# Holding back early score units in one batch, ranking an addition first, and moving six small copies, in a fused attention and mixer kernel

## The chip, the cores and the metric

The kernel runs on one core of one Trainium2 chip. A core has TensorE (PE) for matrix products, VectorE (DVE), ScalarE (ACT), GpSimd (POOL) and SyncE (SP). Each engine works through its own queue in order. SP and POOL also start transfers (DMA) here. The metric is the device time of one execution in microseconds (us), as the median of several runs. Lower is better.

## The reference

Eight batches of 3008 rows are computed. An attention-like stage without softmax gates u, and a mixer (first over the rows, "tokens", then over the columns, "channels") follows it:

```python
scores = (1.0 / S) * np.matmul(z, z.transpose(0, 2, 1))   # z: 8 x 3008 x 64
attn = np.maximum(scores, 0.0) ** 2
x = u * np.matmul(attn, v)                                # u, v: 8 x 3008 x 256
h = np.maximum(x.transpose(0, 2, 1) @ w_tok1, 0.0) @ w_tok2      # 256 tokens inside
u2 = x + h.transpose(0, 2, 1)
out = u2 + np.maximum(u2 @ w_ch1, 0.0) @ w_ch2            # 1536 channels inside
```

## The kernel before

**Tiles and blocks.** The rows of a batch are cut into six blocks of 512 (the last has 448). A block (b, q) is the 512 query rows q of batch b; it needs the squared relu of its scores against all six groups g of 512 key rows. The scores are symmetric, so a block (b, q) with q > g is not computed again: the tile of (b, g, q) is turned by DMA transposes (`flip`, L562) and used a second time. Tiles on the diagonal (`triangle`) are computed only on and above the diagonal, and their lower part is filled by three small transposes (`flip_tiles`, L554).

**Score units.** The list `units` (L332) holds every (b, q, g) in the order in which it is to be scored, in two halves `pr`, each of which is two matmuls of 512 columns (L465) into one pair of PSUM banks. ScalarE applies the relu (L503, on the diagonal L491) into one of six `at` tiles, and VectorE squares it in place (L511, on the diagonal L542). From there on a tile is ready for the product with v (`av_matmul`, L692), or for its transposes into one of eleven `fl` tiles. `score_run` sends units to TensorE in the order of the list; `can_score` says how many of the next ones may go (their z is turned, and an `at` tile is free in the plan).

**PSUM.** From the second block on there are four pairs of banks (`ring`). A block holds two of them for its accumulators acc0 and acc1, a score unit, a token product, a channel product or a mixer output holds one until an engine has emptied it.

**The end of a block.** `finish` (L804) copies the upper half of an accumulator on ScalarE (L820), adds it to the lower half on VectorE (L826), which frees the pair, and multiplies by u (`gate`, L846). SP turns the result (`turn_x`, L884), and VectorE makes four differences of it (`x_sums`, L921), which the fast form of the token product reads.

**The mixer of a batch.** `tok1` (L1029) sums up the token product over the batch; `tok2` (L1086) multiplies back into six tiles h_ps, and `add` (inside `tok2`, L1095, the token addition) adds each to xT on VectorE; `ch1` (L1143) makes the hidden channels hp from xT, and ScalarE, at times VectorE, applies the relu into h2pre (L1181, L1183). The second channel product is either plain (`ch2`, L1365) or in a form with seven instead of eight products (`product`, L1279), for which VectorE makes sums hsum of h2pre (`make_sums`, L1222 to L1234); seven collections (L1316) add the products to the result ro. The last 64 rows of two batches share one plain product: `keep_ends` (L1151) copies them from h2pre into the tile hs, with six copies for each batch, on GpSimd (L1155).

**The order.** All this is interleaved by a planner that runs when the program is built (the loop at L1742). It keeps an estimate of TensorE's time (`pe[0]`) and of when each engine is free, and picks for TensorE a score run, a half of an AV group, or a mixer piece. Work of VectorE, ScalarE and SP is put in by `push(engine, ready, busy, lat, fn, first)`; `next_op` (L372) takes the operation with the smallest key `(start, -first, ready)`, so `first` decides between operations that could start at the same time. The squares (L493, L505), the sums and the token addition have first=0, the accumulator's addition and the gate first=1. What an operation's function emits beside it, as `keep_ends` does, is put into the queues at the point at which the planner issues that operation, without a cost of its own. The engines' real order is then fixed, and the semaphores make it safe.

`goals` (L1733) sets when mixer pieces may come. Batch 0's token sum (L1029) comes before block (1,2), and its six token products with the channel work of its first three tiles before block (1,3). The rest of batch 0's mixer comes before block (2,0), together with the first half of batch 1's, and so on from batch to batch. At the boundary that the change touches, TensorE's order is: last products of block (1,2), six token products mixed with the first channel products, plain channel products, then blocks (1,3), (1,4) and (1,5), and the next mixer stretch.

The lines in the loop that choose the number of units to be scored:

```python
runs = blk is not None and blk.whole
most = RING if runs else 1
n = can_score(done_units, most)
slots = sorted(d.t for d, _ in ring if d.t is not None)
n_now = min(n, len(slots))
```

Of the kernel before, what the change touches and what calls it, by code (L numbers as in the profile page):

```python
# [57 lines left out]
def kernel(  # L58
# [11 lines left out]
    nc = tc.nc  # L70
    B, S, D = u.shape
# [9 lines left out]
    NQ = (S + QW - 1) // QW  # L81
# [8 lines left out]
    first = ctx.enter_context(ExitStack())  # L90
# [97 lines left out]
    def bank_pair(slot, name):  # L188

        if slot == RING and not last_psum:  # L190
            first.close()
            last_psum.append(ctx.enter_context(
                tc.tile_pool(name="last_psum", bufs=1, space=bass.MemoryType.PSUM)))
        pool = psum if slot < RING else last_psum[0]
        return pool.tile([P, 2, QW], F32, tag=f"ps{slot}", name=name, bufs=1)
# [122 lines left out]
    def key_order(b, q):  # L318

        direct = [g for g in range(LAST) if direct_block(b, q, g)]  # L320
        flipped = [g for g in range(LAST) if not direct_block(b, q, g)]
        first = (b, q) == (0, 0)
        made = direct + [LAST] if first else direct[:1] + [LAST] + direct[1:]
        order = []
        while direct or flipped:
            order += direct[:1] + flipped[:1]
            del direct[:1], flipped[:1]
        order.insert(LAST if first else 2, LAST)
        return made, order


    units = [((b, q, g), pr) for b in range(B) for q in range(NQ)  # L332
             for g in key_order(b, q)[0] for pr in range(GK // 2)]
# [22 lines left out]
    ring = [(Done(0.0), i) for i in range(RING)]  # L356
# [7 lines left out]
    def push(engine, ready, busy, lat, fn, first=0, room=(), done=None, frees=()):  # L364
        op = Op(ready, busy, lat, fn, first, room, done, frees)
        waiting[engine].append(op)
        return op.done

    def has_room(names):
        return names() if callable(names) else all(live[n] < ROOM[n] for n in names)  # L370
# [65 lines left out]
    def can_score(first_unit, most):  # L436

        n, at = 0, live["at"]
        for (b, q, g), pr in units[first_unit:first_unit + most]:
            if (b, q) not in turned or (b, g) not in turned:  # L440
                break
            at += pr == 0
            if at > ROOM["at"]:
                break
            n += 1
        return n
# [493 lines left out]
    def take_slot():  # L940
        slot = min((s for s in ring if s[0].t is not None), key=lambda s: s[0].t)
        ring.remove(slot)
        return slot[1], slot[0].t
# [55 lines left out]
    def add_mixer(b):  # L999
# [80 lines left out]
        def tok2(q, end):  # L1080
            slot, _ = take_slot()
            W = widths[q]
            h = bank_pair(slot, "h_ps")
            for dh in range(DT):
                for th in range(2):
                    nc.tensor.matmul(  # L1086
                        h[:, dh, :W], st["a"][:, th, dh * P:(dh + 1) * P],
                        w_tok2_sb[:, th, q * QW:q * QW + W], start=(th == 0), stop=(th == 1))

            def add(t):  # L1090

                xT = xTs[b, q]
                n = full_tiles[q]
                to = xT[:, :, :n * P].rearrange("p h (t s) -> p h t s", t=n)
                nc.vector.tensor_add(  # L1095
                    to, to, h[:, :, :n * P].rearrange("p h (s t) -> p h t s", t=n))
                if n * P < W:
                    to = xT[:, :, n * P:W]
                    nc.vector.tensor_add(to, to, h[:, :, n * P:W])
                if W < QW and b % 2:  # L1100

                    nc.gpsimd.tensor_copy(xT[:, :, W:], xT[:, :, W - TAIL:W])
                    t += 0.5
                u_done[q].t = t
                st["turned", q] = push("sp", t, 1.25, 5.5, lambda t: turn_u2(q, t), first=1,
                                       room=lambda: has_room(("us",)) and (
                                           q <= HALF or goal[0] > (b, 1 + HALF)))
            ring.append((push("dve", end + 0.21, 1.12, 1.25, add), slot))

        def turn_u2(q, t):  # L1110
            live["us"] += 1
# [18 lines left out]
        def ch1(q, c2, borrowed, end):  # L1130
            slots = [take_slot()[0] for _ in range(1 + ((b, q, c2) == VERY_LAST))]
            W = widths[q]
            xT = xTs[b, q]
            if c2 % 2 == 0:
                live["h2"] += 1
                st["h2", q, c2 // 2] = sb.tile(
                    [P, 4, QW], BF16, tag="h2", name="h2pre", bufs=ROOM["h2"])
            hps = [bank_pair(slot, "hp") for slot in slots]
            hp = hps[0]
            for r in range(2):  # L1140
                cc = 2 * c2 + r
                for dc in range(DT):
                    nc.tensor.matmul(  # L1143
                        hps[r % len(hps)][:, r, :W], w_ch1_sb[:, dc, cc * P:(cc + 1) * P],
                        xT[:, dc, :W], start=(dc == 0), stop=(dc == DT - 1))
            h2 = st["h2", q, c2 // 2][:, 2 * (c2 % 2):2 * (c2 % 2) + 2, :]

            def load(e):
                return max(free[e], end) + sum(op.busy for op in waiting[e])

            def keep_ends():  # L1151
                if c2 == 0 and b % 2 == 0:
                    pair["hs"] = sb.tile([P, CHT, P], BF16, tag="hs", name="hs", bufs=1)
                r = b % 2 * TAIL
                nc.gpsimd.tensor_copy(  # L1155
                    pair["hs"][:, 2 * c2:2 * c2 + 2, r:r + TAIL], h2[:, :, W - TAIL:W])

            if (b, q, c2) == VERY_LAST:
                landed, freed = [], Done()

                def evacuate_part(r, t):
                    if r:
                        nc.scalar.activation(h2[:, r, :W], hps[1][:, r, :W], ACT.Relu)
                    else:
                        nc.vector.tensor_single_scalar(h2[:, r, :W], hp[:, r, :W], 0.0, AX.max)
                    landed.append(t)
                    if len(landed) == 2:
                        h2_done[q, c2].t = freed.t = max(landed)
                        keep_ends()

                for r, engine, at, busy in ((0, "dve", end - 0.18, 0.62), (1, "act", end + 0.21, 0.5)):
                    push(engine, at, busy, busy + 0.16, lambda t, r=r: evacuate_part(r, t))
                ring.extend((freed, slot) for slot in slots)
                release("xT", xT_uses[q])
                return
            on_act = load("act") + 0.92 < load("dve") + 1.15 + (b > 0)

            def evacuate(t):
                recent[0] = h2[:, 0, :1]
                if on_act:  # L1180
                    nc.scalar.activation(h2[:, :, :W], hp[:, :, :W], ACT.Relu)  # L1181
                else:
                    nc.vector.tensor_single_scalar(h2[:, :, :W], hp[:, :, :W], 0.0, AX.max)  # L1183
                if q == NQ - 1:
                    keep_ends()
                if fast(q) and c2 % 2:
                    if borrowed and q == HALF and b < B - 1:
                        late_sums.append(lambda t: make_sums(q, c2 // 2, t))
                    else:
                        make_sums(q, c2 // 2, t)  # L1190
            engine, busy = ("act", 0.92) if on_act else ("dve", 1.15)
            ring.append((push(engine, end + 0.21, busy, busy + 0.16, evacuate,
                              done=h2_done[q, c2]), slots[0]))
            if c2 == CHT // 2 - 1:
                release("xT", xT_uses[q])
# [150 lines left out]
        def fast(q):  # L1346

            return (b > 0 or q >= HALF) and (b, q) != (B - 1, NQ - 1)
# [62 lines left out]
        for q in range(NQ):  # L1411
            heads.append(Piece(0.784, [x_done[b, NQ - 1], xd_done[b, q], tok_mix_done],
                               lambda end, q=q: tok1(q, end),
                               opens=q < NQ - 1, closes=q > 0, key=(b, 0), joins=q == 0 and b > 0))
        for q in range(NQ):
            heads.append(Piece(4 * column_time(widths[q]), [a_done, tok2_done[q]],
                               lambda end, q=q: tok2(q, end), key=(b, 1)))
# [318 lines left out]
    done_units = 2  # L1736
# [5 lines left out]
    while cur[0] is not None or heads or tails:  # L1742
# [4 lines left out]
        blk = cur[0]  # L1747
# [11 lines left out]
        runs = blk is not None and blk.whole  # L1759
        most = RING if runs else 1  # L1760
        n = can_score(done_units, most)
        slots = sorted(d.t for d, _ in ring if d.t is not None)
        n_now = min(n, len(slots))
        ts = FAR
# [115 lines left out]
```

## Time and profile before

| what | value |
|---|---|
| median of three runs | 1122.46 us (1120.7 to 1124.12) |
| the profiled execution | 1119.13 us |
| its span, first to last instruction | 1117.2 us |
| TensorE busy | 1108.2 us, 99% |
| VectorE busy | 782.6 us, 70% |
| ScalarE busy | 655.4 us, 59% |
| GpSimd busy | 164.6 us, 15% |
| mean granted clock of TensorE | 0.999 |
| HBM, read and written | 65.40 and 24.64 MB, 81 GB/s |

A line of the timeline gives the start from the beginning of the span, the duration, the engine, the source line and the operation, the tile written and the tiles read, the shape, and in brackets the idle time of the engine before it with what ended it. A group "x4" is four instructions of one kind that follow each other. The matmuls are pipelined: one of 512 columns is listed with some 0.37 us, but the next one starts about 0.22 us after it, or about 0.11 us in the products L465 and L692, where two use half of the array each. So the starts tell the pace, not the durations. In the same way ScalarE's relu of 1024 elements is listed with 1.02 us, and three of them in a row take 2.85 us. Batch 0's blocks and the first blocks of batch 1 fill the span up to about 128 us; the first mixer stretch of batch 0 lies from there to 168 us; blocks (1,3) to (1,5) follow until 201 us; then the next mixer stretch. That one lasts until 272 us. From there on the blocks of a batch and a mixer stretch follow each other, with a period of some 136 us, and the last batch's mixer ends near 1112 us.

### The profile page before, as it was taken

To read this page: it belongs to the slowest core of one execution; us is meant where nothing else is said; L and a number is where in the kernel's file an instruction comes from. 1 tells how busy PE (TensorE), PEld (TensorE's weight loads), DVE (VectorE), ACT (ScalarE), POOL (GpSimd) and SP (SyncE) were. 2 spreads that over 40 slices of the span, in tenths; PEclk is the share of its full clock that TensorE was granted. 3 is DMA by queue.
4 is the path that set the end of the run, shared out by engine and by line. 5 is a ranking of instruction groups with operands and counts; after the bars stand their busy time and mean duration, and the time that the engine had idled before them with its cause. 6 is when DMAs were issued, how large, how long until landed. Compare 5 with 4: busy or idle time off the path is not lost.

```text
span 1117.2 us, 26931 instructions
## 1 busy us (share of the span) xinstructions
PE 1108.2 (99%) x10965; PEld 682.2 (61%) x10965; DVE 782.6 (70%) x1850; ACT 655.4 (59%) x816; POOL 164.6 (15%) x388
## 2 busy tenths in 40 slices
PE   9999999999999999999999999999999999999998
PEld 3444466766557665576555865557655676556776
DVE  6889756875758757588565885578756787557764
ACT  8998525535855458545675456653676536743453
POOL 5320110221003110031000311003200220000000
PEclk9999999999999999999999999999999999999999
DMA  9999954687877959779596897968978678685123
GB/s 178 173 182 160 201 115 109 123 178 139 179 130 151 184 132 185 131 147 210 124 184 117 151 196 143 167 123 162 192 150 172 115 152 168 132 159 105 53 71 82
DMA packets 466155, 165.51 MB, mean 148 GB/s; under 512 B 433072, under 2 KB 449008, under 8 KB 466032
## 3 DMA queue, kind: packets, MB, share of 16 engines
q1 hardware_dynamic: 436640, 131.11, 56.5%
q0 software_dynamic: 28880, 32.32, 20.4%
q8 instruction: 85, 1.39, 0.5%
q10 hardware_dynamic: 512, 0.38, 0.1%
q14 instruction: 38, 0.31, 0.1%
HBM read 65.40 MB, written 24.64 MB: 81 GB/s over the span
## 4 chain that ended last, share of the span: by engine, by line
PE 97%; DMA 1%; DVE 1%; ACT 0%; issue 0%; POOL 0%; ACTq 0%
PE acc L692 41%; PE hp L1143 22%; PE xb L1279 10%; PE zb L1279 7%; PE sc L465 6%; PE a_ps L1029 3%; PE h_ps L1086 3%; PE op L1365 3%; PE first_acc L609 1%; DMA fl<-at 1%; DMA v_sb<-in_v_dram 0%; DVE a_f L1045 0%; PE wp L205 0%; DVE xT L1095 0%; DVE a_f L1049 0%; DVE a_f L1057 0%
## 5 line engine op out<-in xcount | busy, mean ns | idle before, releaser
L1181 ACT ACTIVATE h2pre<-hp 128x1024 bf16<-128x1024 f32 (+1 forms) x276 | 268.6, 1007 | 258.4 <-PE hp L1143 172.7
L692 PEld LDWEIGHTS <-v_sb 64*128 64x128 bf16 x4418 | 244.4, 94 | 213.0
L692 PE MATMUL acc<-at,v_sb 64*128 64x512 bf16 (+1 forms) x2738 | 339.9, 374 | 0.0
L503 ACT ACTIVATE at<-sc 128x1024 bf16<-128x1024 f32 (+1 forms) x290 | 288.1, 1027 | 79.7 <-PE sc L465 72.7
L511 DVE TENSOR_TENSOR at<-at 128x1024 bf16<-128x1024 bf16 (+1 forms) x290 | 198.6, 688 | 114.6 <-ACT at L503 110.0
L1143 PE MATMUL hp<-xT,w_ch_sb 128*128 128x512 bf16 (+1 forms) x1152 | 273.3, 375 | 0.1
L692 PE MATMUL acc<-fl,v_sb 64*128 64x512 bf16 (+1 forms) x1680 | 191.1, 367 | 0.0
L1143 PEld LDWEIGHTS <-w_ch_sb 128*128 128x128 bf16 x1152 | 106.2, 98 | 99.8 <-issue 3.0
L465 PE MATMUL sc<-zT 64*128 64x512 bf16 (+1 forms) x732 | 131.6, 359 | 0.1
L1279 PEld LDWEIGHTS <-hsum 128*128 128x128 bf16 x1944 | 115.9, 98 | 16.8
L1279 PEld LDWEIGHTS <-h2pre 128*128 128x128 bf16 x1458 | 89.1, 98 | 19.3 <-issue 1.2
L820 ACT COPY cp<-acc 128x512 f32<-128x512 f32 (+1 forms) x94 | 54.8, 583 | 62.8 <-PE acc L692 50.4
L826 DVE TENSOR_TENSOR cp<-acc,cp 128x512 f32<-128x512 f32 (+1 forms) x94 | 63.5, 676 | 35.4 <-ACT cp L820 34.6
L491 ACT ACTIVATE at<-sc 128x512 bf16<-128x512 f32 (+3 forms) x152 | 56.2, 443 | 47.2 <-PE sc L465 44.5
L1222 DVE TENSOR_TENSOR hsum<-h2pre 128x512 bf16<-128x512 bf16 (+1 forms) x132 | 52.7, 403 | 39.0 <-ACT h2pre L1181 38.5
L1316 DVE TENSOR_TENSOR ro<-xb,u_sb 128x256 f32<-128x256 f32 (+1 forms) x132 | 52.8, 400 | 24.0 <-PE xb L1279 22.2
L542 DVE TENSOR_TENSOR at<-at 128x512 bf16<-128x512 bf16 (+3 forms) x152 | 41.7, 322 | 39.8 <-ACT at L491 39.8
L1279 PE MATMUL xb<-w_mix_sb,hsum 128*128 128x128 bf16 x972 | 68.6, 219 | 0.0
L465 PEld LDWEIGHTS <-zT 64*128 64x128 bf16 x732 | 42.4, 94 | 41.5 <-issue 3.9
L124 POOL CAST mark<-at 128x1 f32<-128x1 bf16 x24 | 7.7, 320 | 377.0 <-DVE at L511 377.0
L846 DVE TENSOR_TENSOR xT<-cp,uT 128x512 bf16<-128x512 f32 (+1 forms) x94 | 62.4, 664 | 0.8
L1095 DVE TENSOR_TENSOR xT<-xT,h_ps 128x1024 bf16<-128x1024 bf16 (+1 forms) x48 | 54.7, 1173 | 4.7 <-PE h_ps L1086 4.6
(88 smaller groups left out, 988.0 us busy)
## 6 DMA issues: line engine op xcount, KB each, us to landing
out_dram<-ro SPq DMA_DIRECT2D x37, 512.0 KB, 2.9
v_sb<-in_v_dram POOLq DMA_DIRECT2D x40, 256.0 KB, 4.6
ur<-in_u_dram POOLq DMA_DIRECT2D x40, 256.0 KB, 5.1
w_tok_sb<-in_moe_w_tok_dram POOLq DMA_DIRECT2D x10, 256.0 KB, 10.7
zs<-in_z_dram POOLq DMA_DIRECT2D x35, 64.0 KB, 3.6
at<-at SPq DMA_TRANSPOSE x114, 2.4
out_dram<-ro SPq DMA_DIRECT2D x7, 256.0 KB, 2.2
fl<-at SPq DMA_TRANSPOSE x105, 4.2
```

What stands on the lines that cost most here:

```text
L465: nc.tensor.matmul(sc[:, r, c0:c1], zT[h, k:k + P], zT[h, m + c0:m + c1], start=True, stop=True)
L491: nc.scalar.activation(a3[:, i, c0:c1], sc[:, r, c0:c1], ACT.Relu, scale=inv_S)
L503: nc.scalar.activation(view, sv, ACT.Relu, scale=inv_S)
L511: nc.vector.tensor_mul(view, view, view)
L692: nc.tensor.matmul(o, vs[blk.b, g][rows, i, dh * P:(dh + 1) * P], rhs, start=(dh, h) not in blk.begun, stop=stop, skip_group_check=True)
L820: nc.scalar.copy(cp[:, :W], acc[:, 1, :W])
L826: nc.vector.tensor_add(cp[:, :W], acc[:, 0, :W], cp[:, :W])
L846: nc.vector.tensor_mul(xT[:, dh, :full * P].rearrange("p (t s) -> p t s", s=P), acc[:, :full * P].rearrange("p (t s) -> p t s", s=P), uT[: ...
L1095: nc.vector.tensor_add(to, to, h[:, :, :n * P].rearrange("p h (s t) -> p h t s", t=n))
L1143: nc.tensor.matmul(hps[r % len(hps)][:, r, :W], w_ch1_sb[:, dc, cc * P:(cc + 1) * P], xT[:, dc, :W], start=(dc == 0), stop=(dc == DT - 1))
L1181: nc.scalar.activation(h2[:, :, :W], hp[:, :, :W], ACT.Relu)
L1279: nc.tensor.matmul(to[:, i * P:(i + 1) * P], lhs, weights[:, c2, :], start=(first_use and c2 == 0 and i == 0), stop=(c2 == CHT // 2 - 1), ...
```

## The change

Three edits. (1) While TensorE's current block is in batch 1, a score unit is only sent if it belongs to the current block or to the next one; units further on are held (for block (1,5), the next one is (2,0)). (2) The token addition is pushed with first=2 instead of 0, ahead of everything else on VectorE in the planner's ties. (3) In the last batch, the six copies into hs are VectorE's instead of GpSimd's.

```diff
@@ tok2 @@
-            ring.append((push("dve", end + 0.21, 1.12, 1.25, add), slot))
+            ring.append((push("dve", end + 0.21, 1.12, 1.25, add, first=2), slot))
@@ keep_ends @@
                 r = b % 2 * TAIL
-                nc.gpsimd.tensor_copy(
+                copier = nc.gpsimd if b < B - 1 else nc.vector
+                copier.tensor_copy(
                     pair["hs"][:, 2 * c2:2 * c2 + 2, r:r + TAIL], h2[:, :, W - TAIL:W])
@@ the planner's loop @@
         n = can_score(done_units, most)
+        if n and blk is not None and blk.b == 1:
+            b, q, _ = units[done_units][0]
+            if b * NQ + q > NQ + blk.q + 1:
+                n = 0
         slots = sorted(d.t for d, _ in ring if d.t is not None)
```

The changed kernel has the same instructions on TensorE and SP as before. One hp relu goes from VectorE to ScalarE, and the six copies from GpSimd to VectorE. TensorE's order differs in two places only: at the end of block (1,2), where the first half of unit (1,4,4) is no longer scored ahead of the mixer stretch, and in blocks (1,3) to (1,5), where the units of (1,5) and (2,0) come later. On the other engines the order differs in the same stretch, at the token additions of each batch (one sum hsum, L1227, comes after the last addition instead of before it), and at the six copies.

## The prediction

> **What bounds the kernel now.** I read the page's busy shares and its chain of waits first, then what TensorE waited for, and then the timeline of each engine around the places where the order of the changed kernel differs. On the page, TensorE is the bound, at full clock:
>
> ```profile
> span 1117.2 us, 26931 instructions
> PE 1108.2 (99%) x10965; PEld 682.2 (61%) x10965; DVE 782.6 (70%) x1850; ACT 655.4 (59%) x816; POOL 164.6 (15%) x388
> PEclk9999999999999999999999999999999999999999
> PE 97%; DMA 1%; DVE 1%; ACT 0%; issue 0%; POOL 0%; ACTq 0%
> ```
>
> So only TensorE's own stalls can be won, and only new ones can be lost. What it waited for, in the whole span, is a handful of waits, three of them at one line, the token product L1086:
>
> ```profile
> PE h_ps L1086 <- ACT at L491: 0.9, 1, 0.9
> PE h_ps L1086 <- DVE xT L1095: 0.7, 1, 0.7
> PE xb L1279 <- DVE ro L1316: 0.7, 4, 0.2
> PE h_ps L1086 <- DVE cp L826: 0.2, 1, 0.2
> ```
>
> The timeline of TensorE shows where (start, duration, engine, line, operation, count, idle before it):
>
> ```profile
> 128.09 1.90 PE L1086 MATMUL h_ps<-w_tok_sb,a_sb 128*128 128x512 bf16 x8
> 130.85 1.02 PE L1086 MATMUL h_ps<-w_tok_sb,a_sb 128*128 128x512 bf16 x4 [0.86 <-ACT at L491]
> 132.06 1.02 PE L1086 MATMUL h_ps<-w_tok_sb,a_sb 128*128 128x512 bf16 x4 [0.18 <-DVE cp L826]
> 133.19 1.02 PE L1143 MATMUL hp<-xT,w_ch_sb 128*128 128x512 bf16 x4
> 134.92 1.02 PE L1086 MATMUL h_ps<-w_tok_sb,a_sb 128*128 128x512 bf16 x4 [0.71 <-DVE xT L1095]
> 135.78 1.03 PE L1143 MATMUL hp<-xT,w_ch_sb 128*128 128x512 bf16 x4
> 136.64 0.92 PE L1086 MATMUL h_ps<-w_tok_sb,a_sb 128*128 128x448 bf16 x4
> 137.40 2.97 PE L1143 MATMUL hp<-xT,w_ch_sb 128*128 128x512 bf16 x13
> ```
>
> Four matmuls of 512 columns take 0.86 us from start to start (134.92 to 135.78), of 448 columns 0.76 (136.64 to 137.40). From 128.09 to 137.40 there are seven groups of the first kind and one of the second: 7 x 0.86 + 0.76 = 6.78 us of work in 9.31, so 2.5 us of stall (1.04 before 130.85, 0.35, 0.27, and 0.87 before 134.92). What made it is on ScalarE and VectorE:
>
> ```profile
> 129.82 0.98 ACT L491 ACTIVATE at<-sc 128x512 bf16<-128x512 f32 x2 [2.22 <-DMA fl<-at]
> 130.69 0.59 ACT L820 COPY cp<-acc 128x512 f32<-128x512 f32 x1
> 130.45 0.74 DVE L542 TENSOR_TENSOR at<-at 128x512 bf16<-128x512 bf16 x2 [1.52 <-ACT at L491]
> 131.31 0.69 DVE L826 TENSOR_TENSOR cp<-acc,cp 128x512 f32<-128x512 f32 x1
> 131.92 1.21 DVE L1095 TENSOR_TENSOR xT<-xT,h_ps 128x1024 bf16<-128x1024 bf16 x1
> 133.05 0.69 DVE L846 TENSOR_TENSOR xT<-cp,uT 128x512 bf16<-128x512 f32 x1
> ```
>
> The relu of unit (1,4,4), scored last before the mixer, waits 2.22 us for an at buffer that a transpose still reads. Behind it stand the copy of the second accumulator on ScalarE, and on VectorE the unit's squares, that accumulator's addition, and the first token addition. Two of the four PSUM pairs stay taken meanwhile.
>
> **The hold.** In TensorE's order the first half of (1,4,4) moves behind the mixer stretch, to the place where its second half is; the two score matmuls cost the same there (0.2 us), so this moves work and removes none. Its place is now free: ScalarE's copy L820 no longer waits. The accumulator's last matmuls end near 128.0; copy to 128.6; VectorE, after L511 (127.64) and L846 (128.25), starts L826 near 128.9 and the first L1095 near 129.5 instead of 131.92. The second L846 (0.69) now stands behind all six additions. Additions follow each other every 1.14 us (132.00 to 133.13 in the chain; the group of five took 5.47). So the pair of addition k is free at 130.6, 131.8, 132.9, 134.1. TensorE at rate would ask, with three pairs free at the start: fourth h_ps at 130.5 (pair of the accumulator, free at 129.6), first hp 131.4 (130.6), fifth h_ps 132.2 (131.8), next hp 133.1 (132.9), last h_ps 134.0 (134.1, or the first hp's pair, relu done by 133.6). Each is met with 0.1 to 0.9 us in hand: the stall goes, -2.5 us. From below: if additions start 1 us later than this, each of these asks waits in turn, about 1.0 us in all comes back, -1.5. I take -2.4.
>
> What is late next: in batch 1 the units of two blocks ahead are no longer scored early. In the changed order, the blocks (1,3) and (1,4) run nearly without scores, and all twelve units of (2,0) stand inside block (1,5), 11.2 us at rate (94 matmuls of 448 columns, two to 0.187, and the scores). ScalarE has there two copies left from (1,4) (0.59 each), the triangle pair (1.52 for four, row 171.40), ten relus at 0.93 (two back to back took 1.95 at 169.52) and two copies of 0.53: 13.1 us, so it falls behind by up to 1.9, and it then takes all six of the hp relus that follow, where VectorE took one before. Two pairs are for scores: a relu starts 0.46 after its score (184.26 to 184.72) and a pair is asked for again two units, 1.92 us, later, against 0.46 + 1.02 = 1.48, so the lag is taken up by 0.4 us per pair and by the first accumulator's copy, which stands ahead of the last two relus. Ends: 0 and +1.9 us; nearest to the row of 169.52, I take +0.2.
>
> The transposes move too. On SP's queue the first two of (1,4,4)'s transposes (135.81 and 139.80, 1.2 us each) leave their place beside the two u_sb transposes and come after the mixer stretch; those of (1,5,5) pass behind two x_pair transposes, those of (2,0,0) behind five and one uT. They are due: (1,4,4) is scored 12 us and (1,5,5) 14 us before TensorE reads it, against about 5 us for relu, squares and three transposes (2.4 to landing); (2,0,0) is not read before 270 us. POOL's loads keep their order. Cost 0, cover 6 us or more of (1,3)'s and (1,4)'s products; past it each microsecond would be TensorE's.
>
> **The rank.** first=2 decides ties on VectorE only. Beyond the place above, one sum L1227 (0.42) changes sides with the last token addition in batches 1 to 7: at 240.71 it filled time in which the addition waited for TensorE. The sums' first reader is at 246.84, five microseconds later. Cost 0, bounds -0.1 and +0.1 in each of seven, all hidden.
>
> **The copies.** The six hs copies leave POOL (0.30 each, idle otherwise) for VectorE. No row shows this copy on VectorE; bounds: 0.22 (L542 at 128x128) and 0.42 (L1316), I take 0.22 as the shape is the same, 0.14 of it start to start. Worse is where they stand: written at the relu's issue, each waits for its relu with VectorE's later work behind it. The first two stand before and amid the sums of the last block:
>
> ```profile
> 1097.67 2.64 ACT L1181 ACTIVATE h2pre<-hp 128x1024 bf16<-128x1024 f32 x3 [0.46 <-PE hp L1143]
> 1099.85 0.42 DVE L1316 TENSOR_TENSOR ro<-xb,u_sb 128x256 f32<-128x256 f32 x1
> 1101.08 0.83 PE L1279 MATMUL xb<-w_mix_sb,hsum 128*128 128x128 bf16 x12
> ```
>
> The three relus end at 1098.7, 1099.5 and 1100.3. L1222 (1098.73 before) waits behind the first copy to 1099.7, L1231 follows at 1100.0, the second copy at 1100.35, L1227 at 1100.5, and L1316 on xb, which TensorE's 1101.08 needs, runs 1100.95 to 1101.4: about +0.35 us. The other four wait in gaps that VectorE had anyway (1.00 before 1101.95, 1104.05 and 1106.14); the last lets L1165 end 0.35 later, at 1107.6, and its reader is the eleventh matmul after 1106.70, at 1107.8. Ends 0 and +0.8; I take +0.35.
>
> **Sum.** -2.4 + 0.2 + 0 + 0.35 = -1.85, say -1.9 us. The profiled execution took 1119.13 (span 1117.2 and 1.9 around it), below the median 1122.46 of three runs between 1120.7 and 1124.12. Against the profile this gives 1117.2, against the median 1120.6; I forecast 1120.6, 0.17% less. What counts as different is 0.3%, 3.4 us, so this is no change that would show.
>
> **The rivals.** (1) *The additions stay the bound.* If VectorE's six additions of 1.2 us, not the blocked relu, set this place, half the stall stays: for it speaks that 134.92 waited for L1095 itself; against it that in batch 1 the same products run from 232.65 to 240.32 at rate beside the same additions. -1.2 + 0.2 + 0.35: 1121.8.
> (2) *The wait comes back on VectorE in batch 1 (slower).* In the changed order L921, which waits for the first x_pair transposes, stands ahead of the addition L826 that frees the first accumulator of block (1,4). The transposes may issue when block (1,4) begins, 8.6 us before that accumulator ends (80 matmuls at 0.108); with L921's four steps ahead of the addition, a landing of 8 us is still in time. Landings of x_pair took 2.7 to 16.8 us, 4.2 at the median; from there on, each microsecond is one of TensorE's, since its second score of (2,0) needs that pair. A landing like the worst gives +8.8 - 1.9: 1129.4; one of 14 us, 1126.6. Against it: in this stretch x_pair landed in 2.8.
> The Trainium skill (TensorE: Matmul & The Clock Gate, section HAM oscillation) says that gaps over some 3.4 us let TensorE's clock fall to half; no run here shows it, the longest wait in the list being 1.2 us. By it, such a gap would cost up to 1.7 us more (my estimate, half of one such window).
> (3) *More is won (faster).* If the copies cost nothing and the lag is hidden, -2.5 is all there is by the list of waits: 1120.0. Under 1119.1 it comes only with the spread of the runs, 1.7 us to either side.
> (4) *It does not do what it says.* If the squares were not ahead of the additions for long anyway, rank changes nothing; that is already so in my sum, the hold does the work.
>
> **How the numbers follow.** Forecast 50%, rival 1 20%, rival 2 12%, rival 3 18%. Forecast and rival 1 lie within 0.3% of the median, with a run spread that puts a few of them below 1119.1; rival 3 lies 0.9 us from that bound, and half of it falls beyond. With a little more for winnings that the list of waits does not show, faster 0.22, within 0.65, slower 0.13. The range goes from 1117.6 (all of 2.5 won, and 2.4 of spread) to 1125.0 (lag +1.9 and copies +0.8 over a stall half kept, plus spread, or the first microseconds of rival 2).
>
> **What would show it.** Right: L1086 to L1143 in one run near 128 us without idle time, no L491 between 128 and 168, the first L1095 near 129.5, and the second L846 behind the last; block (1,5) with a score before each eight matmuls and ScalarE busy without gaps to about 2 us past it; near 1101 a wait of xb L1280 for ro L1317 of some 0.3 us. Wrong: waits of TensorE for L826 or for the relus near 190 to 200 us, VectorE idle on L921's transposes, or any difference of whole microseconds between 205 and 1095 us, where I expect none.

## The result, and the profile after

The changed kernel took 1116.68 us (median of 22 runs, 1115.63 to 1122.43). The kernel before, run beside it 22 times, took 1120.01 (1118.30 to 1125.86). The ratio of the comparison is 0.9974 with a 95% interval of 0.9962 to 0.9985 (the two medians alone would give 0.9970; here and below the ratios of the comparisons are used, which differ from those of the medians by up to 0.1%): 0.26% less, under the 0.3% that was set as what can be told from no change, though its interval lies wholly below 1. The profiled execution had a span of 1114.0 us, against 1117.2 before. Its page, first the span, TensorE's row and the shares of the chain of waits:

```profile
span 1114.0 us, 26933 instructions
...
PE 1108.1 (99%) x10965; PEld 675.6 (61%) x10965; DVE 780.5 (70%) x1855; ACT 655.1 (59%) x817; POOL 162.7 (15%) x382
...
PE 97%; DVE 1%; ACT 1%; issue 1%; POOL 0%; DVEq 0%; POOLq 0%; ACTq 0%
```

TensorE's busy time is what it was (1108.1 against 1108.2); 3.2 us that it did not work are gone. The list of TensorE's waits (total, number, longest) has lost all three entries of L1086 and got two more small waits for ro. One edit adds a line above it, so L1316 is now L1317, and so on:

```profile
PE wp L205 <- DVE zero L1535: 1.2, 1, 1.2
PE xb L1280 <- DVE ro L1317: 1.0, 6, 0.2
```

The stall at the token products is gone. The timeline of after at the same place:

```profile
127.79 3.63 PE L1086 MATMUL h_ps<-w_tok_sb,a_sb 128*128 128x512 bf16 x16
127.90 0.58 ACT L820 COPY cp<-acc 128x512 f32<-128x512 f32 x1 [0.38 <-PE acc L692]
...
128.76 0.68 DVE L826 TENSOR_TENSOR cp<-acc,cp 128x512 f32<-128x512 f32 x1
129.37 6.60 DVE L1095 TENSOR_TENSOR xT<-xT,h_ps 128x1024 bf16<-128x1024 bf16 x6
131.25 1.03 PE L1143 MATMUL hp<-xT,w_ch_sb 128*128 128x512 bf16 x4
132.12 1.03 PE L1086 MATMUL h_ps<-w_tok_sb,a_sb 128*128 128x512 bf16 x4
...
134.60 3.62 PE L1143 MATMUL hp<-xT,w_ch_sb 128*128 128x512 bf16 x16
...
136.08 0.68 DVE L846 TENSOR_TENSOR xT<-cp,uT 128x512 bf16<-128x512 f32 x1
```

No line of TensorE has a bracket, so it never waited here. ScalarE's copy starts when the accumulator is done, the first token addition starts at 129.37 and the six run in one piece, with the second L846 behind them.

But TensorE's gain is not the whole of it. Setting each matmul of the two traces beside its like gives this course of the difference, after minus before:

```
up to 128 us       -0.30  of it -0.21 two score products that come later now
at 128 to 136 us   -2.50  the stall
by 201 us          +0.17  the two score products, with a small shift
at 201 us          +0.30  products of the channel stage wait for a PSUM pair
at 627 and 764 us  +0.30, +0.34  products xb wait for VectorE's ro
at 1100 us         +0.18  the same, behind the copies on VectorE
end of the last matmul: 1112.10 before, 1110.58 after, -1.52
end of the span:        1117.17 before, 1113.96 after, -3.2
```

Half of the 3.2 us lies behind the last matmul: 5.06 us from there to the end before, 3.38 after. No term of the prediction is there. The chain of waits ends at VectorE's last addition in both, and names nothing later; this is its last piece, before and then after:

```profile
1112.14 0.42 DVE res L1400
```

```profile
1110.62 0.42 DVE res L1401
```

From the end of that piece it is 4.6 us to the end of the span before (1117.17 less 1112.56) and 2.9 after (1113.96 less 1111.04). What runs there is on a line outside the kernel's function, the one that closes the program. The list of that line's instructions by engine's queue (number, shortest, median and longest in ns, first and last start), GpSimd's row, before and then after:

```profile
L1875 POOLq DRAIN  x3: 45/93/8898, 1107.5 to 1116.9; - x3
```

```profile
L1880 POOLq DRAIN  x3: 45/102/8960, 1055.3 to 1113.7; - x3
```

The first of GpSimd's three drains takes 8.9 us and begins with GpSimd's last instruction. Before, that was the last hs copy at 1107.50, so the drain ended at 1116.38 and the span 0.8 us later; SyncE had seen the last output land by 1114.6. In both profiles the drain ends 8.58 us after the end of GpSimd's last instruction. After, GpSimd's last work is a copy L1102 at 1055.36, its drain is over by 1064.3, and the span ends 0.8 us behind SyncE's last wait at 1113.2.

### The profile page after: what moved, and what is told of

It is laid out like the page before. It is cut to its first block, busy times and chain, and to the rows that moved or that the text cites. A ratio compares the mean times of both kernels' runs of the same rounds, so it can differ in the third digit from the quotient of the medians.

```text
span 1114.0 us, 26933 instructions
## 1 busy us (share of the span) xinstructions
PE 1108.1 (99%) x10965; PEld 675.6 (61%) x10965; DVE 780.5 (70%) x1855; ACT 655.1 (59%) x817; POOL 162.7 (15%) x382
## 4 chain that ended last, share of the span: by engine, by line
PE 97%; DVE 1%; ACT 1%; issue 1%; POOL 0%; DVEq 0%; POOLq 0%; ACTq 0%
PE acc L692 41%; PE hp L1143 21%; PE xb L1280 10%; PE zb L1280 7%; PE sc L465 6%; PE h_ps L1086 4%; PE a_ps L1029 3%; PE op L1366 3%; PE first_acc L609 1%; DVE a_f L1045 0%; ACT h2pre L1182 0%; PE wp L205 0%; ACT at L503 0%; POOL hs L1156 0%; DVE at L511 0%
## 5 line engine op out<-in xcount | busy, mean ns | idle before, releaser
L692 PEld LDWEIGHTS <-v_sb 64*128 64x128 bf16 x4418 | 238.0, 94 | 219.3
L1143 PE MATMUL hp<-xT,w_ch_sb 128*128 128x512 bf16 (+1 forms) x1152 | 273.5, 375 | 0.1
L1143 PEld LDWEIGHTS <-w_ch_sb 128*128 128x128 bf16 x1152 | 106.2, 98 | 99.8 <-issue 3.0
L826 DVE TENSOR_TENSOR cp<-acc,cp 128x512 f32<-128x512 f32 (+1 forms) x94 | 63.5, 675 | 42.3 <-ACT cp L820 41.8
L491 ACT ACTIVATE at<-sc 128x512 bf16<-128x512 f32 (+3 forms) x152 | 56.1, 444 | 45.4 <-PE sc L465 45.0
L1223 DVE TENSOR_TENSOR hsum<-h2pre 128x512 bf16<-128x512 bf16 (+1 forms) x132 | 52.2, 400 | 37.7 <-ACT h2pre L1182 35.9
L1317 DVE TENSOR_TENSOR ro<-xb,u_sb 128x256 f32<-128x256 f32 (+1 forms) x132 | 52.6, 399 | 21.9 <-PE xb L1280 20.2
L846 DVE TENSOR_TENSOR xT<-cp,uT 128x512 bf16<-128x512 f32 (+1 forms) x94 | 62.4, 664 | 0.8
L1095 DVE TENSOR_TENSOR xT<-xT,h_ps 128x1024 bf16<-128x1024 bf16 (+1 forms) x48 | 54.6, 1172 | 4.7 <-PE h_ps L1086 4.6
```

The costliest lines, as they stand in the source:

```text
L491: nc.scalar.activation(a3[:, i, c0:c1], sc[:, r, c0:c1], ACT.Relu, scale=inv_S)
L692: nc.tensor.matmul(o, vs[blk.b, g][rows, i, dh * P:(dh + 1) * P], rhs, start=(dh, h) not in blk.begun, stop=stop, skip_group_check=True)
L826: nc.vector.tensor_add(cp[:, :W], acc[:, 0, :W], cp[:, :W])
L846: nc.vector.tensor_mul(xT[:, dh, :full * P].rearrange("p (t s) -> p t s", s=P), acc[:, :full * P].rearrange("p (t s) -> p t s", s=P), uT[: ...
L1095: nc.vector.tensor_add(to, to, h[:, :, :n * P].rearrange("p h (s t) -> p h t s", t=n))
L1143: nc.tensor.matmul(hps[r % len(hps)][:, r, :W], w_ch1_sb[:, dc, cc * P:(cc + 1) * P], xT[:, dc, :W], start=(dc == 0), stop=(dc == DT - 1))
```

## The experiments

The theory to be tried was: the hold takes away the stall, with or without the rank; the copies, by leaving GpSimd, take away 1.7 us of the end; the small waits come of the hold (201 us), of the copies (1100 us) and of transfers (627 and 764 us). All kernels ran beside the kernel before, and all ratios are to it; its medians beside the three groups of runs were 1119.10, 1119.09 and 1119.81 us. Below, "the stretch" is the time from the first token product to the first plain channel product behind this place (L1365), and "the end" the time from the end of the last matmul to the end of the span. Some expectations count the end from the start of the last matmul instead: their 5.4 and 3.7 us are the 5.06 and 3.38 of this text.

**The hold alone.**

```diff
         n = can_score(done_units, most)
+        if n and blk is not None and blk.b == 1:
+            b, q, _ = units[done_units][0]
+            if b * NQ + q > NQ + blk.q + 1:
+                n = 0
```

> The kernel before with the hold alone (rank and copies as before). Theory A (the hold takes away TensorE's stall at the token products, the copies take away the tail): the stall of 2.3 to 2.6 us between 128 and 137 us is gone, about 0.3 us comes back near 201 us, and from the last matmul to the end it is 5.4 us as before, so 2.0 us less than before (ratio 0.998). Theory B (the additions' rank does the work at the stall): half of the stall or more is still there, 0 to 1 us less. Theory C (the shorter tail of the changed kernel is chance, not the copies): the tail can come out anywhere between 3.7 and 5.4 us.

Measured: 1118.2 us, ratio 0.9988 (0.9976 to 0.9999). The span was 1116.5 and the end 5.07 us, as before. The stretch took 12.56 us, against 14.49 before and 11.99 in the changed kernel: 1.93 us of the stall are gone, 0.57 are still there. The timeline of this kernel shows what they wait for:

```profile
130.25 1.21 DVE L1095 TENSOR_TENSOR xT<-xT,h_ps 128x1024 bf16<-128x1024 bf16 x1
131.38 0.69 DVE L846 TENSOR_TENSOR xT<-cp,uT 128x512 bf16<-128x512 f32 x1
...
131.98 5.47 DVE L1095 TENSOR_TENSOR xT<-xT,h_ps 128x1024 bf16<-128x1024 bf16 x5
133.25 1.02 PE L1086 MATMUL h_ps<-w_tok_sb,a_sb 128*128 128x512 bf16 x4 [0.41 <-DVE xT L1095]
```

Without the rank the second L846 stands between the first token addition and the second, and the fifth set of token products waits for the latter. So by these profiles theory A holds for most of the stall, and B for a fifth of it. The time fell by 0.12%, less than the 0.2% of theory A, and the interval nearly reaches no change.

**The copies alone.**

```diff
-                nc.gpsimd.tensor_copy(
+                copier = nc.gpsimd if b < B - 1 else nc.vector
+                copier.tensor_copy(
```

> The kernel before with the last batch's six small copies on VectorE and nothing else. Theory A (GpSimd's closing drain of 8.9 us, which starts behind its last copy, holds the end of the program; with the copies on VectorE it starts at about 1055 us and is over long before): from the last matmul to the end 3.7 us in place of 5.4, about 0.2 us more on TensorE near 1100 us, so 1.5 us less in all (ratio 0.9987); GpSimd's drain starts near 1055 us and still takes 8.9 us. Theory B (what the prediction said: the copies only push VectorE's additions): tail 5.4 us, 0.2 to 0.35 us more (ratio 1.0002 to 1.0003).

Measured: 1118.22 us, ratio 0.9988 (0.9977 to 1.0000). The end was 3.37 us, GpSimd's long drain began at 1056.3 and took 8.96, and TensorE lost 0.18 us at 1100. By the trace that is theory A; the interval of the time reaches to no change. This kernel's order of instructions near 130 us is that of before, and yet the stretch took 13.40 us, 1.1 less than in the first profile: the stall has a part that is not in every execution. That part lies in the transposes: the one that the relu L491 waits for was issued at 119.52 us here and at 120.65 in the first profile, took 9.0 and 9.1 us to land, and the relu waited 1.12 us in place of 2.22.

**The rank alone.**

```diff
-            ring.append((push("dve", end + 0.21, 1.12, 1.25, add), slot))
+            ring.append((push("dve", end + 0.21, 1.12, 1.25, add, first=2), slot))
```

> The kernel before with the additions' rank of 2 and nothing else. In TensorE's order four products of the channel stage (L1143) move ahead of three sets of token products (L1086), and VectorE's additions L1095 close up. Theory A (the stall comes of the score units that were drawn in ahead, whose multiplications stand in VectorE's queue, and the rank does not move them): within 0.5 us of before. Theory B (the rank does the work): 1 to 2.3 us less, the waits of L1086 for VectorE's L1095 gone. Theory C (products moved ahead of token products delay the additions further): 0.3 to 1 us more.

Measured: 1119.37 us, ratio 1.0004 (0.9991 to 1.0017): nothing, as theory A has it, though the interval leaves room for 1 us. By the trace the stretch took 13.33 us, so the waits did not vanish; L1143 now waits 0.5 us for L1095. That is 1.2 us less than in the first profile of before but the same as in the run with the copies alone, and the relu L491 waited 1.12 us in both, so it cannot be put down to the rank. The profiled execution was 2.4 us longer than before for another reason: between 105 and 125 us ScalarE waited for late transposes, with TensorE behind it.

```profile
105.86 3.77 ACT L503 ACTIVATE at<-sc 128x1024 bf16<-128x1024 f32 x4 [2.44 <-DMA fl<-at]
```

**Hold and rank** (the changed kernel without its third edit).

> The changed kernel without its third part (GpSimd keeps the copies). TensorE's order is that of the hold alone; VectorE's and SyncE's differ in a few places. Theory A: as the hold alone within 0.3 us, 2.0 us less than before, tail 5.4 us. Theory B (the rank adds something of its own): 0.3 to 1 us below the hold alone. If the two waits of TensorE for VectorE's ro at 627 and 764 us in the changed kernel (0.3 us each) are the course of this kernel, they are here too and in the hold alone; if they are chance of one run, they are in some of these runs and not in others.

Measured: 1117.43 us, ratio 0.9981 (0.9971 to 0.9992). The stretch took 11.99 us, with no wait in it, and the end 5.06 us. The rank is worth 0.57 us beside the hold in the traces; the times agree (1118.2 with the hold alone) but their intervals overlap. This is theory B, within its bounds. The steps at 627 and 764 us against the first profile of before were 0.13 and 0.83 us, and 0.55 and 0 in the hold alone.

**GpSimd's drain, moved.** Two kernels add one small GpSimd instruction to the changed kernel, whose result nobody reads.

```diff
+                if (b, q, c2) == VERY_LAST:
+                    nc.gpsimd.tensor_copy(mark[:, :1], h2[:, 0, :1])
```

> The changed kernel with one instruction more: GpSimd copies one column of the last h2pre (relu of ScalarE ends near 1105.9 us) into a tile that nobody reads. Nothing else moves. Theory A (the program ends 0.8 us behind the later of SyncE's last wait, 1113.2 us in the changed kernel's profile, and GpSimd's drain, 8.9 us long and begun with GpSimd's last instruction): the drain begins near 1106.1 us and ends near 1115.1, so the span is about 1.9 us longer than the changed kernel's, near 1115.9 (and the whole time 0.9990 of before). Theory B (the shorter tail comes of something else, such as fewer GpSimd instructions near the end in total, or chance): within 0.3 us of the changed kernel, tail 3.4 us from the end of the last matmul.

```diff
                         nc.sync.dma_start(out=to, in_=res[r, j, :])
+                    if last and (b, q) == (B - 1, NQ - 1):
+                        nc.gpsimd.tensor_copy(mark[r, :1], res[r, j, :1])
```

> As the run before it, but GpSimd's extra copy of one column takes the last sum of all (VectorE's last addition ends at 1111.0 us in the changed kernel). Theory A (8.9 us of drain from GpSimd's last instruction, wherever it is): the drain ends near 1120.1 us, span near 1120.9, 6.9 us longer than the changed kernel, 1.0035 of before. Theory B: at most the 0.5 us of the copy itself. Theory C (a drain whose length depends on what GpSimd did lately, so that it is short behind one small copy): something between, with a drain well under 8.9 us.

Measured: 1118.95 us, ratio 1.0000 (0.9990 to 1.0010), and 1123.66 us, 1.0044 (1.0032 to 1.0056). In the second, one copy of a single column and the drain's row:

```profile
1114.75 0.19 POOL L1406 COPY mark<-res 128x1 f32<-128x1 f32 x1 [55.38 <-DVE res L1401]
```

```profile
L1882 POOLq DRAIN  x3: 45/93/8790, 1114.7 to 1124.0; - x3
```

The drain ran from 1114.73 to 1123.53 us, and the span ended at 1124.31, again 0.8 later. From the last matmul to the end it took 10.08 us, 6.7 more than in the changed kernel; the whole was higher still because this profiled execution had the late transposes between 105 and 125 us too. In the first one the drain began at 1106.95, where the instruction had waited for VectorE's half of the relu and not for ScalarE's, took 8.79 and ended at 1115.74; from the last matmul to the end it took 5.05 us, 1.7 more. Theory A holds, theories B and C fall: the drain takes 8.8 to 9.0 us whatever GpSimd did before, and counts from its last instruction. The times show it too: both intervals lie wholly above the changed kernel's. For the first kernel the ratios differ by 2.9 us, more than the 1.7 of its end; where the rest comes from is not shown, though its profile has 0.7 us more of waits at 627 and 764 us than the changed kernel's.

**Copies split.** If only the last GpSimd instruction matters, the first copies can stay there.

```diff
-                copier = nc.gpsimd if b < B - 1 else nc.vector
+                copier = nc.gpsimd if b < B - 1 or c2 < 3 else nc.vector
```

> The changed kernel, but the first three of the last batch's six small copies are GpSimd's again and only the last three VectorE's. GpSimd's last copy is then near 1100.8 us. Theory A: its drain ends near 1109.8, before SyncE's last wait, so the tail stays 3.4 us from the end of the last matmul, and the wait of 0.18 us of TensorE near 1099.6 us (the first two copies stand ahead of VectorE's addition into ro) is gone: 0.2 us less than the changed kernel in the same course, too little for the timing, 0.9972 of before. Theory B (any copy of GpSimd in the last batch lengthens the tail): 5.1 us of tail, 1.5 us more than the changed kernel.

Measured: 1115.79 us, ratio 0.9971 (0.9961 to 0.9982). The drain ran from 1100.55 to 1109.45 us, hidden; the end was 3.38 us; TensorE's 0.18 us near 1099.5 were gone, and no other step of 0.1 us from 30 us on was there. Theory A, to the tenth of a microsecond in the trace; the times cannot tell it from the changed kernel. The drain's row:

```profile
L1880 POOLq DRAIN  x3: 45/93/8897, 1100.5 to 1113.5; - x3
```

**A narrower hold**, with the split copies.

```diff
-        if n and blk is not None and blk.b == 1:
+        if n and blk is not None and blk.b == 1 and blk.q == 2:
```

> As the run before it, and the hold acts only while the block in work is (1,2), where the stall was, so that the end of block (1,5) keeps its old order. Theory A: the 0.3 us that TensorE waits near 201 us for a PSUM slot is gone (before had none there), and the stall near 130 us stays away; with the copies split 0.5 us less than the changed kernel, 0.9970 of before. Theory B (the later blocks' hold is needed too, because what was held in block (1,2) is drawn in too early in the next ones and delays the batch's last block): a new wait between 140 and 205 us of 0.3 us or more.

Measured: 1116.05 us, ratio 0.9983 (0.9966 to 0.9999), and the spread was wide (1114.97 to 1125.99). In the trace the stall stayed away (11.99 us), and the step of 0.30 near 201 us was gone with no new wait: theory A. The place in the changed kernel, for comparison:

```profile
199.73 0.22 DVE L851 TENSOR_TENSOR xT<-cp,uT 128x64 bf16<-128x64 f32 x1
200.03 0.53 ACT L820 COPY cp<-acc 128x448 f32<-128x448 f32 x1 [0.69 <-DVE xT L851]
200.46 5.62 ACT L1182 ACTIVATE h2pre<-hp 128x1024 bf16<-128x1024 f32 x6
```

The accumulator's copy waits for a cp buffer that VectorE's L851 frees, its PSUM pair comes free that much later, and the products of the channel stage that need the pair start 0.30 us late.

**Repeats.** To see what differs between executions of one kernel, before was profiled once more, and the changed kernel and the narrow hold with split copies ran once more.

> The kernel before once more, for a second profile of it. Theory A (the stall near 130 us has a part that varies from one execution to the next: it was 1.1 us shorter in the run with the copies alone, whose order there is that of before): the time from the last score pair ahead of the token products (126.9 us in the first profile) to the first of the 24 products of the channel stage behind them differs from the first profile's by 0.5 us or more, or the wait of L1086 for ScalarE's at L491 (0.9 us) is gone. Theory B (the shorter stall there came of the copies): the same 2.3 to 2.6 us as in the first profile. The tail is 5.1 us from the end of the last matmul in either.

> The changed kernel once more. Theory A (the 0.3 us waits of TensorE for VectorE's ro near 627 and 764 us follow the landing of the transfer out_dram<-ro, which varies by execution): they differ from 0.30 and 0.34 us by 0.1 us or more in this profile. Theory B (they belong to this kernel's course): 0.30 and 0.34 us again. Tail 3.4 us from the end of the last matmul; ratio near 0.9974 of before.

> The kernel with the narrow hold and the split copies once more, beside the changed kernel on the same chip, since its first interval was wide. If the two waits that it lost (0.18 us near 1099, 0.3 us near 201 us) are all that differs: 0.5 us less than the changed kernel, 0.9970 of before; if its order opens it to larger delays by late transfers, its quarter of slowest times lies above the changed kernel's by 1 us or more.

Before again: one run, 1119.71 us, stretch 14.65 us with the wait of 1.0 for L491, end 5.07 us. So theory B has its numbers here, but not its reason: the run with the copies alone and the run with the rank alone show 13.4 and 13.3, and the copies are 960 us later. The relu waited 2.38 us here. The stall is worth 1.4 to 2.7 us, by the execution. After again: 1116.83 us, ratio 0.9975 (0.9965 to 0.9986), end 3.38 us, and the waits at 627 and 764 us were 0.12 and 0 more than in the first profile of before, not 0.30 and 0.34: theory A. This profile has a step of 0.5 us near 149 us that the changed kernel's first one has not: VectorE's addition L1383 waited 4.09 us for the landing of out_dram<-res, and a product L1143 waited for the addition. In before again the one at 627 us was 0.33. This is how it looks in the changed kernel's first profile:

```profile
625.68 0.29 DVE L1223 TENSOR_TENSOR hsum<-h2pre 128x256 bf16<-128x256 bf16 x1 [0.71 <-POOL hs L1156]
...
626.57 0.83 PE L1280 MATMUL xb<-w_mix_sb,hsum 128*128 128x128 bf16 x12 [0.16 <-DVE ro L1317]
```

The bracket names GpSimd's copy, which the sum does not read; in the run of hold and rank it names the transfer out_dram<-ro, whose landing frees the sum's buffer (both tiles are of the pool fl). That transfer took 4.8 us to land here and 4.4 in before. At 764 us the like one took 3.1 us in before, 4.8 in the changed kernel, 5.3 in hold and rank and 5.5 in the first kernel with a GpSimd copy added, and TensorE's steps there were 0, 0.34, 0.83 and 0.97 us. Narrow hold again: 1115.81 us, ratio 0.9966 (0.9954 to 0.9979), 1115.20 to 1116.64, so the wide spread did not come back. Against the changed kernel (0.9975 in the same comparison) it is lower in the median by 1 us, with intervals that overlap: it beats before clearly, the changed kernel only in what its trace no longer has, 0.48 us of waits.

## Why the prediction was wrong

The forecast was no change, which is what came by the bound of 0.3%, but the time lay below the range. Two things put it there, one of the two an error of the working: the copies' term (1.85 us, +0.35 where the traces show -1.5) and the base (2.45 us). Together they are 4.3 us, and the time was missed by 3.9.

**The term that failed: "The copies".** The six copies were costed where they arrive, at VectorE and TensorE: +0.35, with 0 as the best end. Where they leave was called "idle otherwise" and not looked at further. Behind that stands the premise "only TensorE's own stalls can be won": half of the 3.2 us was won behind TensorE's last matmul. Alone the copies measured 0.12% less, with an interval that ends at 1.0000; the traces show what they do: -1.68 at the end of the program, +0.18 near 1100 us. The view that would have shown it was there in the profile of before: 4.6 us between the end of the chain and the end of the span, with GpSimd's last instruction 4.6 us ahead of VectorE's last. The +0.35 itself was too high by half. The order was as told (copy, L1223, L1232, copy, L1228, L1317), but a copy delays what is behind it by 0.10 us where 0.14 was taken (1097.84 to 1097.94), and L1317 came at 1099.09 where it is at 1098.12 with the split copies, 0.97 later for the 1.10 of the working. TensorE's product, due at 1099.34 with the split copies, started at 1099.56: 0.18 came through, the rest being a shift of the two profiles. The copies in the timeline:

```profile
1097.84 0.20 DVE L1156 COPY hs<-h2pre 128x128 bf16<-128x128 bf16 x1 [2.30 <-ACT h2pre L1182]
...
1098.64 0.20 DVE L1156 COPY hs<-h2pre 128x128 bf16<-128x128 bf16 x1
```

**The base.** The forecast was set against 1122.46, the median of three runs. Of the 22 runs of before in the comparison, the median was 1120.01, so 2.45 us of the difference between forecast and result are in the base. From 1120.01 the same sum would give 1118.2, and a range reckoned in the same way would begin at 1115.1, below the result: that would have been luck, with the copies' term still wrong. As a share the forecast (0.9983) lies inside the measured interval, but by a sum in which one term has the wrong sign. With -1.7 + 0.2 in place of +0.35 it would have been -3.7 us against a measured -2.9 (-4.3 to -1.7).

**The hold: right.** -2.4 was taken; in the traces 2.50 (against the first profile of before) and 2.66 (against the second) go with hold and rank, 1.4 where the stall was smaller. Hold and rank together measured 0.19% less (0.08 to 0.29), some 2.1 us, which is -2.4 and +0.3. What would show it came as told: no wait, first L1095 at 129.37 for "near 129.5", the last L846 behind all six. The lag at the end of block (1,5) was 0.30 for 0.2, and its path was another: not the relus but a copy that waits for a cp buffer.

**The rank: mis-attributed.** It was costed at nothing, and L846's place behind the additions was put to the hold. It is the rank's, and worth 0.57 us beside the hold. ("Beyond the place above" leaves room for it, but no number.) In the sum it was counted, under the other name, so the total did not suffer. Rival 4, that the hold does all the work, falls with it.

**The transposes and sums: right**, cost 0: no step of TensorE between 205 and 1095 us is left that is not one of the two waits for transfers, which come and go between executions of one kernel.

**The other rivals.** Rival 1 (additions stay the bound) did not come in the changed kernel; 0.41 us of it shows in the hold alone. Rival 2 (L921 ahead of L826) did not come: no run had a wait for x_pair there. Rival 3 (more is won) had the direction, but not the reason: it took the copies at nothing and left times under 1119.1 to the spread, while 1.7 us more were won at the end. The Trainium skill's rule on gaps (TensorE: Matmul & The Clock Gate, section HAM oscillation) could not be seen at work: the longest wait of TensorE in any of these profiles was 1.8 us, and the mean granted clock was 0.997 or more.

## What to carry to other kernels

When work is moved off an engine, ask what that engine's last instruction then is: look at the stretch between the end of the chain and the end of the span, and at what each engine does when it is done. Where two edits act on one stall, run each alone before giving one of them the credit. Take the base from as many runs as the effect needs: three runs missed the median here by 2.45 us, as much as the largest term of the sum.

## What was not expected of the hardware

GpSimd's drain at the end of the program took 8.79 to 8.96 us in all 13 profiles, whether its last instruction copied one column or a tile. The 0.17 us between these are the last instruction's own length (0.19 to 0.37 us): from its end to the end of the drain it was 8.58 us in each of the 13. The program's end waits for the drain: where the drain was the last to end, the span ended 0.8 us later; in the profiles of before and after the other engines' longest were 2.16 (PEld), 0.58 (ScalarE) and 0.46 us (VectorE). The Trainium skill (VectorE: DVE Perf Modes, section The DRAIN you can't avoid) gives the drains of the runtime's preamble and postamble as some 12 ns, constant, on all five engines. The drains here belong to the line that closes the program, and no run shows whether the page means those too; SyncE's took 7 ns, but for GpSimd's first one the figure would be far too low.

Profiles differ by single waits for transfers: 0 to 0.55 us at 627 and 0 to 0.97 at 764 (against the first profile of before), 1.1 to 1.3 in the stall near 130, 0.5 at 149 in one of 13, up to 1.3 for the first loads of v_sb near 11 us, and in two of 13 profiles 3.4 and 3.5 us between 105 and 125 us, where ScalarE waited 2.4 us for transposes in the row shown above. These waits are of the size of the spread of the runs (1118.30 to 1125.86 for before); that they make it up is not shown, since only profiled runs have a trace.
